# Hash attention and a Strassen-style squared-ReLU layer on one core: which queues carry the second part's transfers, and when they are asked for

## The chip, the cores and the metric

The kernel runs on one core of a Trainium2 chip. The metric is the device time of one execution in microseconds; less is better. Engines are named as in the profile: PE (TensorE), DVE (VectorE), ACT (ScalarE), POOL (GpSimd) and SP (SyncE). PEq, SPq and so on are their instruction queues. A transfer (DMA) is issued by an instruction in the queue of SP, ACT or POOL, in that queue's order, and is then carried out by 16 DMA engines.

## The reference

Attention over 4 x 8 heads of 768 tokens and 64 features, in which a query sees only the keys whose six sign bits equal its own, and then a layer with the square of a ReLU, all in fp32:

```python
q_bits = (np.einsum('bhsd,dk->bhsk', q, proj) > 0)      # the same for k
mask = q_bucket[:, :, :, None] == k_bucket[:, :, None, :]
scores = np.where(mask, scale * np.matmul(q, k.transpose(0, 1, 3, 2)), -1e9)
attn = softmax(scores)
x = (attn @ v).transpose(0, 2, 1, 3).reshape(3072, 512)
h = x @ w_in                                            # w_in 512 x 2048
g = np.maximum(h, 0.0) ** 2
out = g @ w_out                                         # w_out 2048 x 512
```

## The kernel before

**First part** (lines 542 to 596, 0 to 372 us): attention, 16 pairs of heads by 6 key tiles. Its results go to DRAM as `x_all`. Beside it the weights are rounded and stored in DRAM: `w_in_7` holds the seven Strassen factors of `w_in`, `w_out_1` the plain rows of `w_out`. The first chunk of tokens, `x`, is loaded back during this part (`load_x(0)` at step 54), and its sums `t_x` are made.

**Second part** (lines 599 to 942): three chunks of 1024 tokens. A chunk has eight **units** (`hidden`, one for 256 of the 2048 hidden features) and then a **projection** (`project`). A unit is one Strassen product of seven adds (`product`, line 612): 28 matmuls of 512 columns out of the unit's weights `w_unit` (896 KB, two buffers), with ACT copying three intermediate sums out of PSUM (`keep`: one, two, five, three) and DVE making the four squared outputs (`gate`). A projection is seven outer products, each again a Strassen product of seven adds: 49 adds of 8 matmuls of 256 columns, 392 in all. Each add reads a block of factors of 128 x 4 x 128, a **leaf** of 256 KB, loaded six ahead into eight buffers (`load_leaf`, line 753).

The 49 leaves come from `w_out_49` in DRAM, which is made during the first four units of chunk 0: `sums_out(m)` (line 888) loads 1 MB of `w_out_1` into `rows`, ACT copies three quarters of it to `factors`, DVE makes four more quarters and four times seven sums out of them (`sums_a`, line 477), and seven transfers of 448 KB store them. In chunks 1 and 2 each unit also takes the largest absolute value of a sixteenth of q and of k (`peak`, line 652: one buffer `raw_qk`, a load and a reduction, for q and then for k). The maxima set a flag, `slow` (`guard`, line 671), that selects a general version behind the end of the kernel; it isn't taken here.

**What sets the order.** Lines 542 on are under a manual schedule: each engine gets its instructions in the order of the Python code. All loads and stores of the second part stand in SP's queue, in program order, and SP waits at an instruction until its buffers are free and its data is there. So in a unit of chunk 0 SP has: the load of the unit after next (which waits until PE is through with this unit), the load of `rows`, and the seven stores. In chunks 1 and 2 it has the two loads of `raw_qk`, each of which waits for the reduction of the one before; at the last unit the first leaves stand behind them. Between leaves it has the stores of the output, four for each finished block (`put_out`, line 778). At the end of a chunk the next `x` is loaded ahead of the projection, and `sums_x` (line 530, four DVE operations) follows the projection.

Of the kernel before, what the change touches and what calls it, by code (L numbers as in the profile page):

```python
# [8 lines left out]
FP32 = mybir.dt.float32  # L9
# [25 lines left out]
def kernel(  # L35
# [10 lines left out]
    nc = tc.nc  # L46
# [50 lines left out]
    p_c = fast.enter_context(tc.tile_pool(name="p_c", bufs=1, side="right"))  # L97
    ps_s = first.enter_context(tc.tile_pool(name="ps_s", bufs=1, space=PSUM))
# [425 lines left out]
    def load_x(i):  # L524

        x = p_c.tile([P, NFT, NCH], FP32, name="x")
        nc.sync.dma_start(out=x, in_=x_all[:, :, i * NCH:(i + 1) * NCH])
        xs[i] = x, [p_c.tile([P, 2, NCH // 2], FP32, name=f"t_x{n}") for n in range(3)]

# [12 lines left out]
    with tc.manual_schedule():  # L542
# [14 lines left out]
        for u in range(len(steps) + 1):  # L557
# [34 lines left out]
            for f, i in w_steps.get(u, ()):  # L592
                f(i)
            if u == X_0:
                load_x(0)
# [4 lines left out]
        p_i = fast.enter_context(tc.tile_pool(name="p_i", bufs=2, reuse_waits="tile"))  # L600
# [48 lines left out]
        NPK = 16  # L649
        peaks = p_k.tile([P, 2, NPK], FP32, name="peaks")  # L650

        def peak(w, i):

            n = B * H * S * D // P // NPK
            t = p_k.tile([P, n], FP32, name="raw_qk")
            flat = (q, k)[w].rearrange("b h s d -> (b h s d)").rearrange("(p f) -> p f", p=P)
            nc.sync.dma_start(out=t, in_=flat[:, i * n:(i + 1) * n])
            nc.vector.tensor_reduce(  # L658
                out=peaks[:, w, i:i + 1], in_=t, axis=AXL.X, op=ALU.max,
# [28 lines left out]
        w_unit = {}  # L688

        def load_unit(n):  # L690

            if n < NCHUNK * NR:
                r = n % NR
                w_unit[n] = p_i.tile([P, 7, NFT // 2, P], FP32, name="w_unit")
                nc.sync.dma_start(
                    out=w_unit[n].rearrange("p l f c -> p (l f) c"),
                    in_=w_in_7.rearrange("p l f c -> p (l f) c")[:, :, r * P:(r + 1) * P],
                )

        def hidden(i, r):  # L700
# [11 lines left out]
            def gate(out):  # L712
                def put(one, two=None):
                    h = p_r.tile([P, HN], FP32, name="h", bufs=4)
# [38 lines left out]
        def load_leaf(n):  # L753
            if n < 49:
# [3 lines left out]
                nc.sync.dma_start(out=leaves[k, m], in_=w_out_49[OUTER[k][0], :, m])  # L758

        LEAVES, NLEAF = (0, 1, 4, 3, 5, 6, 2), 8  # L760
# [30 lines left out]
        def project(i):  # L791
# [54 lines left out]
            for k in range(7):  # L846
# [27 lines left out]
                )  # L874
                if k == 0:
# [11 lines left out]

        def sums_out(m):

            t = p_1.tile([P, 2, 2, 2, 2, P], FP32, name="rows")  # L890
# [251 lines left out]
```

## Time and profile before

| | us |
|---|---|
| Three runs, median (lowest to highest) | 1024.74 (1024.43 to 1025.59) |
| The profiled execution, whole | 1024.79 |
| Its span in the profile | 1022.9 |
| PE busy | 921.2 (90% of the span) |
| DVE busy | 700.0 (68%) |
| ACT busy | 371.1 (36%) |
| POOL busy | 6.0 (1%) |
| Queue 1 (SP's transfers) | 157.32 MB, 59.3% of 16 engines' span |

The profile is one execution. The profiled time is 1.9 us above its span, and 0.05 us above the median of the runs. The 40-slice view of the span shows PE at nine tenths or more in the first part, from slice 2 to slice 14, and at six tenths in slices 15 to 19, most of chunk 0 of the second part. There the granted TensorE clock is at seven and eight tenths of full speed. A busy PE at half clock is busy twice as long for the same work, so the busy share alone doesn't show the loss; the time of a stage beside the time of the same work at full pace does.

### The profile page before, as it was taken

Reading aid. Unit: us, or ns where it says so; the run is one execution under the profiler, and the core shown is the slowest. Engines: PE = TensorE matmul, PEld = TensorE weight load, DVE = VectorE, ACT = ScalarE, POOL = GpSimd, SP = SyncE. Lnnn points to the kernel's source line nnn. Section 1 sums busy time; section 2 is a strip of 40 time slices with the busy share of each in tenths; the row PEclk is TensorE's granted clock in tenths of the full one; section 3 lists DMA queues with packets and bytes.
Section 4 is the critical chain, followed back from the end, with each engine's and each line's share of the span. In section 5 each row is a group of like instructions: output and inputs, shape, how many; then the busy total and the mean of one; then the engine's idle time right before and its main releaser. Section 6 shows DMA issues by size and latency. Waiting matters only on the chain.

```text
span 1022.9 us, 11731 instructions
## 1 busy us (share of the span) xinstructions
PE 921.2 (90%) x4326; PEld 502.0 (49%) x4326; DVE 700.0 (68%) x1016; ACT 371.1 (36%) x607; POOL 6.0 (1%) x22
## 2 busy tenths in 40 slices
PE   5999999999999966666979998999599999978995
PEld 2334334334334422222448884444488744437884
DVE  2788977998867844544557875657677756676775
ACT  3777776777776712111211111222011122221110
POOL 2000000000000000000000000000000000000000
PEclk9999999999999978777989999999799999998998
DMA  9456885897663233777366563444854735526555
GB/s 185 102 105 134 237 172 108 225 232 202 152 143 109 88 108 108 231 217 226 102 211 192 154 149 86 136 147 133 286 152 131 156 85 154 153 67 194 151 151 109
DMA packets 287007, 158.14 MB, mean 155 GB/s; under 512 B 178016, under 2 KB 250208, under 8 KB 286944
## 3 DMA queue, kind: packets, MB, share of 16 engines
q1 hardware_dynamic: 286880, 157.32, 59.3%
q8 instruction: 36, 0.59, 0.2%
q14 instruction: 27, 0.22, 0.1%
q0 software_dynamic: 64, 0.00, 0.0%
HBM read 119.28 MB, written 38.01 MB: 154 GB/s over the span
## 4 chain that ended last, share of the span: by engine, by line
PE 66%; DMA 19%; DVE 9%; issue 2%; ACT 2%; SPq 2%; DVEq 0%; ACTq 0%
PE acc L621 33%; PE st L381 16%; PE xo L409 13%; DMA raw_qk<-in_q_dram 7%; DMA raw_qk<-in_k_dram 4%; DMA rows<-w_out 3%; PE tot L427 2%; DVE peaks L658 2%; DMA leaf<-w_out 2%; PE hash L322 2%; SPq L786 1%; DVE b L484 1%; DVE h L718 1%; DVE ot L782 1%; DVE t_x L484 1%
## 5 line engine op out<-in xcount | busy, mean ns | idle before, releaser
L386 ACT ACTIVATE e<-st 128x1024 f32<-128x1024 f32 x192 | 145.5, 810 | 90.9 <-PE st L381 90.4
L621 PE MATMUL acc<-x,w_unit 128*128 128x512 f32 x384 | 170.7, 596 | 8.2 <-DMA w_unit<-w_in 8.2
L621 PE MATMUL acc<-t_x,w_unit 128*128 128x512 f32 x288 | 139.1, 636 | 36.4 <-ACT one L628 33.8
L621 PE MATMUL acc<-b,leaf 128*128 128x256 f32 x600 | 138.5, 390 | 28.5 <-DMA leaf<-w_out 28.5
L381 PE MATMUL st<-feat,feat 64*128 64x512 f32 (+1 forms) x768 | 152.6, 489 | 0.0
L409 PE MATMUL xo<-e,v_nat 128*64 128x512 f32 (+1 forms) x768 | 144.9, 498 | 0.2 <-DVE x_t L464 0.2
L621 PEld LDWEIGHTS acc<-b,leaf 128*128 128x128 f32 x600 | 117.5, 196 | 47.8 <-DMA leaf<-w_out 31.0
L621 PEld LDWEIGHTS acc<-x,w_unit 128*128 128x128 f32 x384 | 73.4, 192 | 99.6 <-issue 98.8
L621 PEld LDWEIGHTS acc<-t_x,w_unit 128*128 128x128 f32 x288 | 58.4, 205 | 114.2 <-issue 73.8
L409 PEld LDWEIGHTS xo<-e,v_nat 128*64 128x64 f32 x768 | 46.9, 136 | 86.5 <-issue 84.8
L381 PEld LDWEIGHTS st<-feat,feat 64*128 64x128 f32 x768 | 67.3, 191 | 35.1 <-issue 32.5
L399 DVE TENSOR_TENSOR total<-total,e 128x1536 f32<-128x1536 f32 x48 | 83.7, 1744 | 1.1 <-ACT e L386 1.0
L628 ACT COPY one<-acc 128x512 f32<-128x512 f32 (+1 forms) x45 | 21.9, 486 | 153.9 <-PE acc L621 137.4
L658 DVE TENSOR_REDUCE peaks<-raw_qk 128x1 f32<-128x768 f32 x32 | 30.5, 953 | 68.4 <-DMA raw_qk<-in_k_dram 49.9
L621 PE MATMUL acc<-t,leaf 128*128 128x256 f32 x336 | 75.9, 379 | 0.0
L628 ACT COPY two<-acc 128x512 f32<-128x512 f32 (+1 forms) x45 | 21.9, 487 | 140.3 <-PE acc L621 137.3
L381 PE MATMUL st<-bits,bits 64*128 64x256 bf16 (+1 forms) x384 | 64.2, 331 | 7.4 <-DVE bits L347 5.4
L332 ACT ACTIVATE bits<-hash,lifts 32x384 bf16<-32x384 f32 x120 | 68.7, 573 | 4.9 <-PE hash L322 3.4
L621 PEld LDWEIGHTS acc<-t,leaf 128*128 128x128 f32 x336 | 63.8, 190 | 8.7
L719 DVE SCALAR_TENSOR_TENSOR b<-h 128x512 f32<-128x512 f32 x96 | 64.3, 690 | 2.5
L621 PE MATMUL acc<-b_t,leaf 128*128 128x256 f32 x240 | 54.5, 380 | 6.3 <-DMA leaf<-w_out 6.3
L381 PEld LDWEIGHTS <-bits 64*128 64x128 bf16 x384 | 19.0, 94 | 72.5 <-issue 65.8
(117 smaller groups left out, 808.9 us busy)
## 6 DMA issues: line engine op xcount, KB each, us to landing
leaf<-w_out SPq DMA_DIRECT2D x147, 256.0 KB, 2.8
w_unit<-w_in SPq DMA_DIRECT2D x24, 896.0 KB, 5.4
raw<-in_moe_w_in_dram SPq DMA_DIRECT2D x16, 512.0 KB, 4.3
raw<-in_moe_w_out_dram SPq DMA_DIRECT2D x16, 512.0 KB, 3.7
w_out<-sums SPq DMA_DIRECT2D x16, 448.0 KB, 6.0
v_nat<-in_v_dram SPq DMA_DIRECT2D x16, 384.0 KB, 4.2
x_all<-x_t SPq DMA_DIRECT2D x16, 384.0 KB, 3.0
x<-x_all SPq DMA_DIRECT2D x3, 2048.0 KB, 9.8
```

What stands on the lines that cost most here:

```text
L322: nc.tensor.matmul(out=hashed[pr][h][g * NR_B:(g + 1) * NR_B, 0:HS], lhsT=projs[rows], rhs=feat[pr, w][rows, c * HS:(c + 1) * HS], start=T ...
L332: nc.scalar.activation(out=t[h * D:h * D + NR_B, c * HS:(c + 1) * HS], in_=hashed[pr][h][at, 0:HS], func=ACTF.Sign, scale=HUGE, bias=lifts ...
L381: nc.tensor.matmul(out=st[:, h, 0:hi - lo], lhsT=src[pr, 1][rows, key], rhs=src[pr, 0][rows, lo:hi], start=first, stop=not first,)
L386: nc.scalar.activation(out=e[:, :, lo:hi], in_=st[:, :, 0:hi - lo], func=ACTF.Exp, scale=scale)
L399: nc.vector.tensor_tensor(out=totals[pr], in0=in0, in1=weights[pr, kt][:, :, 0:S], op=ALU.add)
L409: nc.tensor.matmul(out=xo[h * D:(h + 1) * D, lo:hi], lhsT=nat[pr, "v_nat"][:, h, kt * D:(kt + 1) * D], rhs=weights[pr, kt][:, h, lo:hi], s ...
L427: nc.tensor.matmul(out=tot[g * 32:(g + 1) * 32, 0:HS], lhsT=ones, rhs=src[:, h, c * HS:(c + 1) * HS], start=src is totals[pr], stop=src is ...
L484: nc.vector.tensor_tensor(out=out, in0=in0, in1=in1, op=ALU.subtract)
L621: nc.tensor.matmul(out=acc[to], lhsT=a(i), rhs=b(i), start=first and i == 0, stop=last and i == n - 1, skip_group_check=True,)
L628: nc.scalar.copy(out=t, in_=acc[of])
L658: nc.vector.tensor_reduce(out=peaks[:, w, i:i + 1], in_=t, axis=AXL.X, op=ALU.max, apply_absolute_value=True,)
L719: nc.vector.scalar_tensor_tensor(out=out[:, r], in0=h, scalar=0.0, in1=h, op0=ALU.max, op1=ALU.mult)
```

## The change

- The loads of `x`, the stores to `w_out_49` and the loads of `raw_qk` move from SP's queue to POOL's. The loads of leaves move to ACT's queue.
- The buffers `w_unit` are given room from the start, and units 0 and 1 are loaded during the first part, at step 60. The load of the unit after next stands at the end of a unit's work.
- `sums_out` no longer loads `rows` and has ACT copy three quarters of it. `load_rows` has four transfers put the quarters where they are needed (three into `factors`, one into `other`), with two buffers, for m and m + 1 ahead; m + 2 is asked for behind `sums_out(m)`.
- The maxima of q and k are taken in 32 pieces instead of 16, q and k in one buffer and one reduction, two pieces a unit, each loaded two ahead.
- The first five leaves are asked for one unit earlier (at r = 6). Leaves have seven buffers instead of eight, and `h` three instead of four.
- The next `x` is loaded behind the first outer product of the projection, and `sums_x` stands behind the sixth and the seventh one. `guard` stands behind the sixth.

```diff
     def load_x(i):
         x = p_c.tile([P, NFT, NCH], FP32, name="x")
-        nc.sync.dma_start(out=x, in_=x_all[:, :, i * NCH:(i + 1) * NCH])
+        nc.gpsimd.dma_start(out=x, in_=x_all[:, :, i * NCH:(i + 1) * NCH])
...
+            if u == X_0 + SB:
+                for n in range(2):
+                    load_unit(n)
             if u == X_0:
                 load_x(0)
...
-        NPK = 16
+        NPK = 32
...
+        def load_peak(i):
             n = B * H * S * D // P // NPK
-            t = p_k.tile([P, n], FP32, name="raw_qk")
-            flat = (q, k)[w].rearrange("b h s d -> (b h s d)").rearrange("(p f) -> p f", p=P)
-            nc.sync.dma_start(out=t, in_=flat[:, i * n:(i + 1) * n])
+            raw_qk[i] = p_k.tile([P, 2, n], FP32, name="raw_qk", bufs=2)
+            for w in range(2):
+                flat = (q, k)[w].rearrange("b h s d -> (b h s d)").rearrange("(p f) -> p f", p=P)
+                nc.gpsimd.dma_start(out=raw_qk[i][:, w], in_=flat[:, i * n:(i + 1) * n])
+
+        def peak(i):
+
             nc.vector.tensor_reduce(
-                out=peaks[:, w, i:i + 1], in_=t, axis=AXL.X, op=ALU.max,
+                out=peaks[:, :, i], in_=raw_qk.pop(i), axis=AXL.X, op=ALU.max,
...
-                nc.sync.dma_start(out=leaves[k, m], in_=w_out_49[OUTER[k][0], :, m])
+                nc.scalar.dma_start(out=leaves[k, m], in_=w_out_49[OUTER[k][0], :, m])
-        LEAVES, NLEAF = (0, 1, 4, 3, 5, 6, 2), 8
+        LEAVES, NLEAF = (0, 1, 4, 3, 5, 6, 2), 7
...
+                if k == 0 and i + 1 < NCHUNK:
+                    load_x(i + 1)
+                if k > 4 and i + 1 < NCHUNK:
+                    sums_x(i + 1, k - 5)
+                if k == 5 and i + 1 == NCHUNK:
+                    guard()
...
+        def load_rows(m):
+
+            f = p_1.tile([P, 7, 2, 2, P], FP32, name="factors")
+            t = p_1.tile([P, 2, 2, P], FP32, name="other")
+            src = w_out_1[:, m:NFF:NQ].rearrange("p n (h c) -> p n h c", h=2)
+            for o, n, h in ((f[:, 0], 0, 0), (f[:, 1], 2, 0), (t, 0, 1), (f[:, 2], 2, 1)):
+                nc.sync.dma_start(out=o.rearrange("p n h c -> p n (h c)"), in_=src[:, n:n + 2, h])
+            rows[m] = f, t
+
         def sums_out(m):
...
-            for n, a in enumerate((a11, a12, a22)):
-                nc.scalar.copy(out=f[:, n], in_=a)
-            sums_a(a11, a12, a21, a22, *(f[:, 3 + n] for n in range(4)))
-            g = p_1.tile([P, 4, 7, P], FP32, name="sums")
+            f, t = rows.pop(m)
+            sums_a(f[:, 0], f[:, 1], t, f[:, 2], *(f[:, 3 + n] for n in range(4)))
+            g = p_1.tile([P, 4, 7, P], FP32, name="sums", bufs=1)
...
-                nc.sync.dma_start(
+                nc.gpsimd.dma_start(
                     out=w_out_49[:, :, n, m].rearrange("l p e -> p l e"), in_=a
                 )
...
-        p_1 = p_1s.enter_context(tc.tile_pool(name="p_1", bufs=1, reuse_waits="tile"))
+        p_1 = p_1s.enter_context(tc.tile_pool(name="p_1", bufs=2, reuse_waits="tile"))
+        for m in range(2):
+            load_rows(m)
         for i in range(NCHUNK):
             for r in range(NR):
                 hidden(i, r)
-                load_unit(i * NR + r + 2)
                 minus(b_t[:, r], b12[:, r], b11[:, r])
                 if i == 0 and r < NQ:
                     sums_out(r)
-                if i > 0:
-                    for n in range(2):
-                        peak(n, (i - 1) * NR + r)
+                    if r + 2 < NQ:
+                        load_rows(r + 2)
...
-                if r == NR - 1:
+                if r == NR - 2:
                     for n in range(NLEAF - 2):
                         load_leaf(n)
+                load_unit(i * NR + r + 2)
+                for n in range(2):
+                    m = 2 * ((i - 1) * NR + r) + n
+                    if m >= 0:
+                        peak(m)
+                    if 0 <= m + 2 < NPK:
+                        load_peak(m + 2)
```

How the instructions stand, at three places. A name in brackets behind `waits` is a semaphore: DMAHW0 to 7 count the transfers issued by SP and ACT together, DMASW0 to 7 those issued by POOL, the others name an engine.

SP's queue at the beginning of the second part, before: the three loads of weights, the first load of `rows`, the stores of m = 0 and the next unit and rows:

```order
L695 DMA w_unit<-w_in_63 128x14x128 [waits DMAHW5_49]
L695 DMA w_unit<-w_in_63 128x14x128 [waits DMAHW6_49]
L695 DMA w_unit<-w_in_63 128x14x128 [waits DMAHW7_49,DMAHW5_49,PE_49]
L891 DMA rows<-w_out_65 128x4x512 [waits DMAHW0_49,Activation_49]
L903 DMA w_out_66<-factors 128x7x128 [waits DMAHW1_49,DVE_49,Activation_49]
L903 DMA w_out_66<-factors 128x7x128 [waits DMAHW2_49]
L903 DMA w_out_66<-factors 128x7x128 [waits DMAHW3_49]
L903 DMA w_out_66<-sums 128x7x128 [waits DMAHW4_49,DVE_49]
L903 DMA w_out_66<-sums 128x7x128 [waits DVE_49]
L903 DMA w_out_66<-sums 128x7x128 [waits DMAHW6_49]
L903 DMA w_out_66<-sums 128x7x128 [waits DMAHW7_49,DVE_49]
L695 DMA w_unit<-w_in_63 128x14x128 [waits DMAHW0_49,PE_49]
```

The same queue in the changed kernel, from the third load of quarters (m = 2) on; the quarters of m = 0 and 1 stand right ahead of it:

```order
L909 DMA factors<-w_out_65 128x2x256 [waits DMAHW1_49,DMASW5_49,DMAHW6_49,DMASW4_49,DMAHW7_49,DMASW3_49,DVE_49]
L909 DMA factors<-w_out_65 128x2x256
L909 DMA other<-w_out_65 128x2x256 [waits DMAHW0_49]
L909 DMA factors<-w_out_65 128x2x256
L538 DMA w_unit<-w_in_63 128x14x128 [waits DMAHW2_49,PE_49]
L909 DMA factors<-w_out_65 128x2x256 [waits DMASW4_49,DMAHW3_49,DMASW3_49,DMAHW5_49,DMASW2_49,DVE_49]
L909 DMA factors<-w_out_65 128x2x256 [waits DMAHW4_49]
L909 DMA other<-w_out_65 128x2x256
L909 DMA factors<-w_out_65 128x2x256 [waits DMAHW6_49]
L538 DMA w_unit<-w_in_63 128x14x128 [waits DMAHW7_49,PE_49]
L538 DMA w_unit<-w_in_63 128x14x128 [waits DMAHW2_49,DMAHW0_49,PE_49]
```

The stores are gone from the queue and the loads of m = 2 and 3 stand ahead of the loads of units 2 and 3; the first of each four waits for three transfers that POOL issued.

POOL's queue, before, from its last work of the first part to the read of the flag at the end:

```order
L249 TENSOR_TENSOR picks<-ident 128x32 x4
L252 MEMSET which 128x24
L254 MEMSET which 32x12 [waits Pool_49]
L254 MEMSET which 32x12 x3
L971 TENSOR_LOAD slow [waits DVE_49]
```

In the changed kernel, the same place and the stores of m = 0 (the first three are those of `factors`, the other four those of `sums`):

```order
L255 MEMSET which 32x12 x3
L528 DMA x<-x_all 128x4x1024 [waits DMAHW7_49,DMAHW3_49]
L920 DMA w_out_66<-factors 128x7x128 [waits DMAHW6_49,DMAHW7_49,DMAHW1_49,DVE_49]
L920 DMA w_out_66<-factors 128x7x128 x2
L920 DMA w_out_66<-sums 128x7x128 [waits DVE_49] x2
L920 DMA w_out_66<-sums 128x7x128 [waits DMASW0_49]
L920 DMA w_out_66<-sums 128x7x128 [waits DMASW1_49,DVE_49]
L920 DMA w_out_66<-factors 128x7x128 [waits DMAHW3_49,DMAHW2_49,DMAHW5_49,DMASW2_49,DVE_49]
L920 DMA w_out_66<-factors 128x7x128 [waits DMASW3_49]
```

A queue that was empty in the second part now has 28 stores in chunk 0, in groups of seven, and after them the loads of `raw_qk` and `x`.

ACT's queue at the beginning of the first projection, before: the last copy of unit 7 and then the copies of the first two outer products:

```order
L716 COPY h<-acc_3643 128x512 [waits DVE_49,PE_49]
L628 COPY one<-acc_3708 128x256 [waits PE_49]
L628 COPY two<-acc_3708 128x256 [waits PE_49]
L628 COPY five<-acc_3710 128x256 [waits PE_49]
L628 COPY three<-acc_3708 128x256 [waits PE_49]
L812 COPY sum_3704<-acc_3708 128x256 [waits DMAHW2_49,DMAHW6_49,DMAHW1_49,DMAHW7_49,DMAHW0_49,PE_49]
L628 COPY one<-acc_3778 128x256 [waits DVE_49,PE_49]
L628 COPY two<-acc_3778 128x256 [waits DVE_49,PE_49]
L628 COPY five<-acc_3780 128x256 [waits DVE_49,PE_49]
```

The same place in the changed kernel:

```order
L765 DMA leaf<-w_out_66 128x512 [waits DMAHW3_49,DMASW7_49,DMASW6_49]
L643 COPY one<-acc_3707 128x256 [waits PE_49,Activation_49]
L765 DMA leaf<-w_out_66 128x512 [waits DMAHW4_49]
L765 DMA leaf<-w_out_66 128x512 [waits DMAHW5_49]
L643 COPY two<-acc_3707 128x256 [waits PE_49,Activation_49]
L765 DMA leaf<-w_out_66 128x512 [waits DMAHW6_49]
L643 COPY five<-acc_3709 128x256 [waits PE_49,Activation_49]
L765 DMA leaf<-w_out_66 128x512 [waits DMAHW7_49]
L643 COPY three<-acc_3707 128x256 [waits PE_49,Activation_49]
L765 DMA leaf<-w_out_66 128x512 [waits DMAHW0_49]
L765 DMA leaf<-w_out_66 128x512 [waits DMAHW1_49]
L819 COPY sum_3703<-acc_3707 128x256 [waits PE_49]
```

The leaves stand between the copies that PE waits for, and wait for counters that SP's transfers use too.

## Rows read from the trace of the kernel before

**Rows 1.** The page, its first line.

```profile
span 1022.9 us, 11731 instructions
```

**Rows 2.** Busy time of each engine in six stretches, us; then granted clock, DMA share, GB/s.

```profile
371.90:529.80 157.90, 109.85 (x224) 46.88 (x225) 79.79 (x118) 29.66 (x52) 0.00 (x0) 0.83 0.59 173
529.80:618.40 88.60, 86.59 (x393) 75.69 (x394) 63.08 (x88) 11.17 (x30) 0.00 (x0) 0.98 0.65 182
618.40:727.50 109.10, 96.48 (x225) 42.23 (x223) 68.91 (x102) 23.44 (x40) 0.00 (x0) 0.97 0.46 134
727.50:816.30 88.80, 86.81 (x393) 75.90 (x394) 65.03 (x93) 11.18 (x30) 0.00 (x0) 0.98 0.66 182
816.30:925.00 108.70, 96.37 (x224) 42.12 (x223) 68.71 (x102) 23.46 (x40) 0.00 (x0) 0.97 0.41 117
925.00:1014.50 89.50, 87.08 (x394) 75.87 (x394) 65.26 (x95) 11.19 (x30) 0.00 (x0) 0.98 0.62 159
```

**Rows 3.** What TensorE waited for: us in total, times, longest.

```profile
PE acc L621 <- DMA leaf<-w_out: 34.9, 6, 11.4
...
PE acc L621 <- ACT one L628: 33.8, 4, 9.0
...
PE acc L621 <- DMA w_unit<-w_in: 8.2, 1, 8.2
```

**Rows 4.** Chain of waits from 364 to 530: start us, us, what.

```profile
371.45 0.42 PE tot L451 x2
...
380.04 13.67 PE acc L621 x28
...
394.34 8.39 DMA rows<-w_out
...
475.84 47.88 PE acc L621 x104
```

**Rows 5.** The same chain, of the whole span.

```profile
529.80 72.66 PE acc L621 x328
...
632.66 5.98 DMA raw_qk<-in_q_dram
```

**Rows 6.** TensorE in order of time: start, us, line, operation, idle before and releaser.

```profile
405.00 7.97 PE L621 MATMUL acc<-t_x,w_unit 128*128 128x512 f32 x12 [7.87 <-ACT one L628]
...
727.54 2.93 PE L621 MATMUL acc<-b,leaf 128*128 128x256 f32 x6 [11.37 <-DMA leaf<-w_out]
```

**Rows 7.** Busy time from 394 to 464, columns as in rows 2.

```profile
394.00:464.00 70.00, 44.56 (x85) 18.69 (x84) 37.31 (x52) 13.18 (x24) 0.00 (x0) 0.78 0.73 218
```

**Rows 8.** VectorE from 372 to 420 in order of time.

```profile
403.36 0.68 DVE L479 TENSOR_TENSOR factors<-rows 128x512 f32<-128x512 f32 x1
...
406.49 1.09 DVE L479 TENSOR_TENSOR sums<-factors 128x896 f32<-128x896 f32 x1
```

**Rows 9.** DMA issues: queue, count, KB each, median us from issue to landing.

```profile
rows<-w_out SPq DMA_DIRECT2D x4, 1024.0 KB, 8.8
...
w_out<-sums SPq DMA_DIRECT2D x16, 448.0 KB, 6.0
...
w_out<-factors SPq DMA_DIRECT2D x12, 448.0 KB, 4.3
...
leaf<-w_out SPq DMA_DIRECT2D x147, 256.0 KB, 2.8
```

**Rows 10.** DMA issuing instructions of lines 903, 758 and 224: ns min/median/max.

```profile
L903 SPq DMA_DIRECT2D w_out<-sums x16: 1311/1386/1711, 407.7 to 482.9; - x16
...
L758 SPq DMA_DIRECT2D leaf<-w_out x147: 319/320/897, 524.4 to 1009.5; - x147
...
L224 POOL DMA_DIRECT2D projs<-in_proj_dram x2: 522/592/662, 1.7 to 2.4; - x2
```

**Rows 11.** SyncE from 1000 to 1023, and a piece of the chain near it.

```profile
1004.97 4.38 SPq L786 DMA_DIRECT2D out_dram<-ot  x8
...
1003.66 1.99 DMA out_dram<-ot
```

## What was predicted

> **What bounds the kernel now.** The first view is busy time by stage. The second part is six stretches in which PE has the same work three times over: eight units and a projection, for each of three chunks. The first stretch takes 157.9 us where the third and fifth take 109.1 and 108.7 for the same eight units; the projections take 88.6, 88.8 and 89.5 [rows 2]. The second view, the chain of waits, gives the pace without waits: four units in a row in 47.88 us, or 11.97 a unit, and six of the seven outer products of a projection in 72.66 us, or 12.11 each [rows 4, 5]. At that pace eight units are 95.8 us and a projection 84.8, and the second part 3 x (95.8 + 84.8) = 541.8 us. The six stretches are 642.6 us long [rows 2], so 100.8 us are lost: 62.1, 3.8, 13.3, 4.0, 12.9 and 4.7, in their order. This is the most that the change can win; the first part it hardly touches.
>
> What ends the waits, PE's list of them tells: leaves 34.9 us, ACT's copy "one" 33.8 us, the first unit's weights 8.2 us [rows 3]. The middle one isn't ACT's doing. In the chain the load of `rows` comes ahead of it, 8.39 us from 394.34 on, after unit 0 (13.67 us from 380.04 on) was through [rows 4]: SP's queue had the load of unit 2, which waits for unit 0, ahead of `rows`. ACT waits with its copies of `rows`, and the copy "one" that PE needs stands behind them; PE sat idle for 7.87 us before 405.00 [rows 6]. The rest of these 62.1 us is clock: between 394 and 464 the granted clock was 0.78 [rows 7], a mixture of 1.2 and 2.4 GHz after each wait, and unit 0, started after 8.2 us of waiting, took 13.67 us and not 11.97, so a restart costs 1.7 us.
>
> **The change, part by part.**
>
> *Start of chunk 0.* Units 0 and 1 are in place early, so PE may go on after its last product of the first part, which ends at 371.45 + 0.42 = 371.87 [rows 4]. I leave 0.5 us of 8.2, and the clock stays up. In the first part two more loads of 896 KB lie beside work bound by PE, at no cost.
>
> *Units 0 to 3.* ACT's twelve copies go, and the quarters of m = 0 and 1 are loaded before they are needed. But the quarters of m = 2 stand ahead of unit 2's weights in SP's queue and wait until the three `factors` stores of m = 0 have landed. This is the new wait on PE's path. DVE is through with unit 0's gates some 2 us after 384.4; four sums of 0.68 us follow, then four of 1.09 [rows 8]. So the first three stores can be issued at about 389.
>
> What POOL takes to issue one, p, no row shows. The only transfers of POOL took 0.52 and 0.66 us for 64 rows each; a store has 896 pieces, which in proportion is 14 x 0.59 = 8.3 us. SP's issue of the same store took 1.39 us [rows 10]. This is the same transfer, so the nearest row: I take p = 1.4 and keep 0.6 and 8.3 as ends. The Trainium skill ("DMA: Bandwidth & Descriptors", section "Anatomy of one DMA — SWDGE (gpsimd) path") says that POOL's software path can emit many descriptors before their cost shows; no run here shows it yet. That speaks for the low end, with which the sum would be 2.4 us lower.
>
> Three issues end at 393.2, and the last store lands 4.3 us later [rows 9], at 397.5. Four quarters are issued in 4 x 0.32 = 1.3 us (the issue of a leaf, also 256 KB [rows 10]), then unit 2's weights, which land with the quarters in about the 8.8 us that `rows` took beside a unit [rows 9]: 407.6. PE wants them after two units, at 396.3. That is a wait of 11.3 us and 1.7 for the restart. Unit 2 ends at 421. For m = 1 the same steps from 401 give 401 + 4.2 + 4.3 + 1.3 + 8.8 = 419.6 for unit 3's weights: just in time. No quarters stand ahead of later units. DVE's load is 37.31 us in three units, 12.4 each [rows 7], a little above 11.97, and costs about 1 us over four units, the rest being buffered. In all 0.5 + 11.3 + 1.7 + 1 = 14.5 us are left of 62.1, the leaf wait at the chunk's end among what goes, since the leaves are asked for a unit earlier and stand behind no other queue.
>
> *Units of chunks 1 and 2.* PE already keeps pace there; what is lost lies at the end, where the first leaves stand behind the loads of `raw_qk` in SP's queue (a piece of 5.98 us in the chain, one of many [rows 5]): PE waited 11.37 us [rows 6]. On ACT the leaves are free of that. DVE still has two reductions and the last inner sums between the last gate and the third add of the projection; I leave 1.5 us of 13.3 and of 12.9. POOL's four loads a unit, two units ahead, are hidden even at several us each.
>
> *Projections.* The sums of `x` no longer stand between projection and unit, and the cold start goes. But ACT now waits, ahead of copies, for counters shared with SP's output stores. In the last two outer products eight stores take 4.38 us to issue and 1.99 to land [rows 11], behind some 3 us of DVE; PE's cover is three adds of 12.11 / 7 = 1.73 us [rows 5]. That is 4.4 + 2.0 + 3 - 5.2 = 4.2 at most and zero at least; with a little left at the start I take 3.5 each, against 3.8, 4.0 and 4.7. A leaf's issue of 0.32 us, 49 times, is 16 us of an ACT that is busy for 11.2 of 88.6 us [rows 2].
>
> *Sum.* 14.5 + 2 x 1.5 + 3 x 3.5 = 28.0 us remain of 100.8, a gain of 72.8. The profiled execution took 1024.8 us (1022.9 of span [rows 1] and 1.9 around it), within 0.1 of the median, so 1024.8 - 72.8 = **952.0**.
>
> **Rivals.** *POOL is slow.* From 395 (389 and the last landing, 6.0 [rows 9]) all 28 stores take 28 p; ACT meets the first leaves after unit 6 and waits there for all of them, with unit 7's copies behind. Chunk 0 then ends at 395 + 28 p + 13. The forecast has it at 371.9 + 95.8 + 14.5 = 482, so up to p = 2.7 this costs little; at p = 4 it ends at 520, for 990 us. Break-even with before is 482 + 72.8 = 555, or p = 5.25. At 8.3 it ends at 640: **1110 us, slower**. For it speaks the proportion to the 64-row loads, against it SP's 1.39 us.
>
> *The 16 engines are the bound.* From 394 to 464 three units' transfers kept them busy for 0.73 of 70 us [rows 7], 17.0 us a unit, where PE needs 11.97. If they fill up, units 0 to 3 end at 372.4 + 68 = 440.4 and not 433.4: 959 us. The Trainium skill ("DMA: Bandwidth & Descriptors", "Issuing engines are not separate DMA queues") says that several issuing queues share the same engines and save only issue time. By that rule this rival has the upper hand; the trace agrees that the engines weren't full, at 0.73.
>
> *ACT is held up by leaves.* If all nine leaf loads of the last two outer products wait 2.0 us each in turn, a projection loses 18 us and not 3.5: 995 us. Against it: loads and copies alternate, and most stores are long done.
>
> **How the numbers follow.** The forecast has 0.66, with a range of its own from 932 (hardly a stall left in chunk 0) to 972 (twice the stall); the engines as the bound 0.10; POOL between 2.7 and 5.25 us 0.10; ACT held up 0.05; POOL above that 0.09. The range of 930 to 990 leaves out the slow POOL (0.09), part of the middling one and of ACT held up (0.06) and 0.04 of the forecast. Faster is 0.89, within 0.2% (what a measurement of this kernel can tell from no change) 0.02, slower 0.09.
>
> **What would show it.** The stretch of chunk 0 tells most: some 110 us from the first unit to the projection, with one wait of PE for `w_unit` before unit 2 and no wait for ACT's "one". POOL's issue of a store should be near 1.4 us. The waits for leaves at the start of a projection should be gone, and what is left at its end should name ACT. The forecast is wrong if POOL's stores take over 2.7 us each, if PE waits for weights before units 3 to 5 too, or if the granted clock in chunk 0 stays below 0.9.

## The result, and the profile after

The changed kernel takes 955.64 us (953.94 to 956.22), the kernel before in the same session 1024.59: a ratio of 0.9327, 95% interval 0.9308 to 0.9345. Forecast were 952.0 and a range of 930 to 990. The profiled execution took 956.22 us, 1.7 of it around its span.

The page of the changed kernel: its first line, TensorE's line, and in the slices PE and the granted clock.

```profile
span 954.5 us, 11820 instructions
...
PE 904.1 (95%) x4326; PEld 493.7 (52%) x4326; DVE 696.9 (73%) x1016; ACT 364.5 (38%) x595; POOL 69.2 (7%) x117
...
PE   5999999999999999549999999999999999999996
...
PEclk8999999999999999869999999999999999999998
```

Where before five slices stood at six tenths, two at five and four are left, the 17th and 18th: one hole instead of many. The six stretches, cut at the same events as in [rows 2] (columns as there):

```profile
371.20:496.40 125.20, 98.81 (x225) 42.66 (x224) 75.10 (x111) 22.72 (x39) 29.01 (x32) 0.90 0.69 208
496.40:581.70 85.30, 84.91 (x393) 74.23 (x392) 68.12 (x96) 11.75 (x31) 0.76 (x1) 1.00 0.67 190
581.70:678.50 96.80, 96.62 (x226) 42.43 (x225) 63.01 (x98) 22.82 (x39) 14.85 (x28) 1.00 0.50 143
678.50:764.10 85.60, 85.04 (x393) 74.27 (x392) 69.79 (x98) 11.75 (x31) 2.86 (x5) 1.00 0.70 198
764.10:860.40 96.30, 96.30 (x225) 42.47 (x225) 62.95 (x98) 22.82 (x39) 14.87 (x28) 1.00 0.47 134
860.40:945.90 85.50, 85.29 (x395) 74.30 (x393) 68.82 (x102) 11.75 (x31) 0.00 (x0) 1.00 0.59 155
```

At the pace of the prediction (95.8 and 84.8) they lose 29.4, 0.5, 1.0, 0.8, 0.5 and 0.7 us: 32.9 in all, against 100.8 before and 28.0 forecast. Everything after the units of chunk 0 runs at full clock and within 1.1% of the pace. Nearly all that is left is one wait. First two rows of TensorE's waits (us in total, times, longest), then the row of TensorE in order of time in which the longest ends:

```profile
PE acc L636 <- DMA w_unit<-w_in: 25.1, 3, 24.4
...
PE acc L636 <- ACT one L643: 1.4, 3, 0.8
```

```profile
419.72 5.17 PE L636 MATMUL acc<-x,w_unit 128*128 128x512 f32 x8 [24.45 <-DMA w_unit<-w_in]
```

There is no wait for a leaf any more, and ACT's "one" is down from 33.8 to 1.4 us [rows 3]. The wait of 24.45 us is for unit 2. With the restart (8 matmuls in 5.17 us, elsewhere 3.60) it makes 26.0 of chunk 0's 29.4. The chain of waits tells how it came about (start us, us, what):

```profile
388.42 1.91 POOL w_out L920 x2
390.33 6.01 DMA w_out<-factors
...
401.00 18.67 DMA w_unit<-w_in
...
419.72 37.80 PE acc L636 x84
```

and SP's queue in order of time beside it:

```profile
377.41 20.94 SPq L909 DMA_DIRECT2D factors<-w_out  x3
398.40 1.25 SPq L909 DMA_DIRECT2D other<-w_out  x1
399.69 1.21 SPq L909 DMA_DIRECT2D factors<-w_out  x1
401.00 1.39 SPq L538 DMA_DIRECT2D w_unit<-w_in  x1
```

This is the predicted order, step by step: stores of m = 0 by POOL, their landing, the quarters of m = 2 in SP's queue, and only then unit 2's weights. The load itself took 18.67 us, where 8.8 were forecast. The DMA queues between 401.0 and 419.7 (packets, MB, share of the 16 engines' time) show what it shared the engines with:

```profile
q0 software_dynamic: 1002, 3.55, 59.1%
q1 hardware_dynamic: 3659, 2.70, 44.5%
```

The engines were full. POOL's transfers (q0) had three fifths of them, in packets of 3.5 KB, while SP's transfers went in packets of 0.7 KB (2.70 MB / 3659).

### The profile page after: what moved, and what is told of

It reads as the page before. It is cut to its first block, busy times and chain, and to the rows that moved or that the text cites. A ratio compares the mean times of both kernels' runs of the same rounds, so it can differ in the third digit from the quotient of the medians.

```text
span 954.5 us, 11820 instructions
## 1 busy us (share of the span) xinstructions
PE 904.1 (95%) x4326; PEld 493.7 (52%) x4326; DVE 696.9 (73%) x1016; ACT 364.5 (38%) x595; POOL 69.2 (7%) x117
## 4 chain that ended last, share of the span: by engine, by line
PE 88%; DMA 5%; DVE 3%; ACT 1%; issue 1%; SPq 1%; ACTq 0%; POOL 0%; DVEq 0%
PE acc L636 52%; PE st L382 17%; PE xo L410 14%; DMA w_unit<-w_in 3%; PE tot L428 2%; PE hash L323 2%; DMA w_out<-factors 1%; PE tot L452 1%; DVE b L726 1%; ACT bits L333 0%; SPq L909 0%; ACT e L387 0%; DMA k_nat<-in_k_dram 0%; DVE h L725 0%; DVE peaks L677 0%
## 5 line engine op out<-in xcount | busy, mean ns | idle before, releaser
L636 PE MATMUL acc<-b,leaf 128*128 128x256 f32 x600 | 133.0, 379 | 0.0
L636 PE MATMUL acc<-t_x,w_unit 128*128 128x512 f32 x288 | 128.0, 594 | 1.4 <-ACT one L643 1.4
L636 PEld LDWEIGHTS acc<-b,leaf 128*128 128x128 f32 x600 | 113.8, 190 | 17.0 <-issue 1.4
L410 PEld LDWEIGHTS xo<-e,v_nat 128*64 128x64 f32 x768 | 46.9, 136 | 86.5 <-issue 84.8
L636 PEld LDWEIGHTS acc<-t_x,w_unit 128*128 128x128 f32 x288 | 54.3, 190 | 71.9 <-issue 66.3
L725 DVE TENSOR_TENSOR h<-acc,two 128x512 f32<-128x512 f32 x24 | 16.6, 690 | 88.3 <-PE acc L636 88.3
```

Source lines behind the costliest of these rows:

```text
L410: nc.tensor.matmul(out=xo[h * D:(h + 1) * D, lo:hi], lhsT=nat[pr, "v_nat"][:, h, kt * D:(kt + 1) * D], rhs=weights[pr, kt][:, h, lo:hi], s ...
L636: nc.tensor.matmul(out=acc[to], lhsT=a(i), rhs=b(i), start=first and i == 0, stop=last and i == n - 1, skip_group_check=True,)
L725: nc.vector.tensor_tensor(out=h, in0=one, in1=two, op=ALU.add)
```

## The experiments

| Kernel | us, median (lowest to highest) | Ratio to before, 95% interval |
|---|---|---|
| changed kernel | 955.64 (953.94 to 956.22) | 0.9327 (0.9308 to 0.9345) |
| u1_stores_on_sp | 960.78 (959.53 to 962.03) | 0.9371 (0.9347 to 0.9395) |
| u2_leaves_on_sp | 975.51 (974.51 to 976.51) | 0.9514 (0.9492 to 0.9537) |
| u3_peaks_on_sp | 988.16 (986.61 to 989.71) | 0.9646 (0.9624 to 0.9669) |
| u4_units_late | 969.32 (968.83 to 969.81) | 0.9462 (0.9444 to 0.9481) |
| u5_sumsx_late | 961.39 (959.13 to 962.06) | 0.9362 (0.9343 to 0.9382) |
| e1_unit_first | 946.88 (945.89 to 947.64) | 0.9232 (0.9216 to 0.9248) |
| e2_rows_on_pool | 952.35 (950.53 to 953.92) | 0.9292 (0.9270 to 0.9314) |
| e3_whole_rows | 940.19 (937.84 to 942.43) | 0.9179 (0.9157 to 0.9202) |
| e4_whole_rows_pool | 939.39 (936.20 to 942.09) | 0.9160 (0.9131 to 0.9189) |
| e5_seven_sums | 946.47 (946.02 to 946.97) | 0.9226 (0.9210 to 0.9242) |
| e6_seven_sums_pool | 929.92 (929.78 to 932.95) | 0.9072 (0.9050 to 0.9094) |
| e7_seven_sums_short | 950.86 (950.34 to 953.47) | 0.9276 (0.9252 to 0.9300) |

The first five take one part of the change back. The others ask why unit 2 waited and what stood behind that.

### Parts taken back

**u1_stores_on_sp**: the 28 stores to `w_out_49` stay in SP's queue.

```diff
-                nc.gpsimd.dma_start(
+                nc.sync.dma_start(
                     out=w_out_49[:, :, n, m].rearrange("l p e -> p l e"), in_=a
```

> One part of the change undone: the 28 stores go back to SP's queue, everything else as in the changed kernel. If a free queue for the stores matters, it is by what stands behind them: unit 2 is late as before (within 3 us), and units 4 and 5 stand behind stores that wait for DVE until some 448 and 463, so PE waits about 12 us for each: 970 to 985. If only the engines' bandwidth matters, the bytes are the same and the time stays within 4 us of 955.6.

Measured: 5.1 us slower than the changed kernel, less than the one text asks for and more than the other. Two of TensorE's rows in order of time, and the DMA queues from 401.4 to 408.9, where unit 2's load was under way:

```profile
408.93 6.03 PE L636 MATMUL acc<-x,w_unit 128*128 128x512 f32 x8 [12.92 <-DMA w_unit<-w_in]
...
445.18 6.68 PE L636 MATMUL acc<-x,w_unit 128*128 128x512 f32 x8 [7.63 <-DMA w_unit<-w_in]
```

```profile
q1 hardware_dynamic: 3750, 2.40, 111.6%
```

Without a rival queue unit 2's load took 7.5 us and the wait was 12.92: close to the forecast's 8.8 and 11.3. So the forecast had priced the load as if the stores were still in SP's queue. What the stores cost there comes later: unit 4's load stands behind those of m = 2 and goes out only at 436.73, for the wait of 7.63. Moving the stores to POOL exchanged one wait for another and won 5 us.

**u2_leaves_on_sp**: the leaves stay in SP's queue, still asked for a unit earlier.

```diff
-                nc.scalar.dma_start(out=leaves[k, m], in_=w_out_49[OUTER[k][0], :, m])
+                nc.sync.dma_start(out=leaves[k, m], in_=w_out_49[OUTER[k][0], :, m])
```

> One part undone: the leaves go back to SP's queue, still asked for a unit earlier and without loads of q and k in that queue. If those loads were what held the first leaves, only the waits at the end of each projection come back, behind output stores, 2.0 to 2.4 us each, with a little clock: 960 to 965. If the queue itself holds the leaves, the waits of 6 to 11 us at the start of the projections come back as well: 978 or more.

Measured: 19.9 us slower, between the two. SP's queue, and the first of TensorE's waits:

```profile
485.31 12.53 SPq L538 DMA_DIRECT2D w_unit<-w_in  x2
497.94 57.90 SPq L765 DMA_DIRECT2D leaf<-w_out  x34
```

```profile
508.63 7.14 PE L636 MATMUL acc<-b,leaf 128*128 128x256 f32 x32 [2.70 <-DMA leaf<-w_out]
```

Five leaves are out early, but the sixth stands behind the load of unit 9, which goes out only when PE is through with unit 7, at the end of the first row; in chunk 0 that costs PE the wait of 2.70. It is the smaller part of 14.8 us in eight pieces. The other seven, 12.1 us, lie in the last two outer products of the projections, where leaves stand behind eight stores of the output. SP's queue and one of these waits of PE:

```profile
578.41 4.42 SPq L793 DMA_DIRECT2D out_dram<-ot  x8
582.93 0.93 SPq L765 DMA_DIRECT2D leaf<-w_out  x2
```

```profile
585.97 5.20 PE L636 MATMUL acc<-b_t,leaf 128*128 128x256 f32 x16 [2.88 <-DMA leaf<-w_out]
```

So with the loads of `raw_qk` out of SP's queue, it is the output stores that hold the leaves up there, as the first text has it, by more than it forecast.

**u3_peaks_on_sp**: the maxima of q and k as before, in 16 pieces, one buffer, SP's queue.

```diff
-        NPK = 32
+        NPK = 16
...
-                nc.gpsimd.dma_start(out=raw_qk[i][:, w], in_=flat[:, i * n:(i + 1) * n])
+            t = p_k.tile([P, n], FP32, name="raw_qk")
+            nc.sync.dma_start(out=t, in_=flat[:, i * n:(i + 1) * n])
...
+                if i > 0:
+                    for n in range(2):
+                        peak(n, (i - 1) * NR + r)
```

> One part of the change undone: q and k are loaded in SP's queue again, into one buffer, a load and a reduction in turn, 16 pieces each. The leaves stay on ACT. If the wait of 11.4 us that PE had at the start of two projections came only from leaves behind those loads, it stays away: 957 to 960. If DVE, held by the loads, was as late as the leaves, PE waits for DVE's inner sums instead, about 8 us and a restart of 1.7 in each of two chunks: 970 to 978.

Measured: 32.5 us slower, more than either text. A row of the chain, and TensorE's longest wait:

```profile
679.61 13.12 DMA raw_qk<-in_q_dram
```

```profile
698.73 4.64 PE L636 MATMUL acc<-t,leaf 128*128 128x256 f32 x10 [14.88 <-DVE t L485]
```

The leaves, on ACT, came in time. It is DVE that stood still, at a reduction that waited for its load, with the sums that PE needs queued behind. The loads come one after the other, since there is one buffer and SP issues each behind that of a unit. This one took 13.12 us, where no load of `raw_qk` took over 6.4 in the kernel before: POOL had issued the 2 MB of the next `x` at 679.25. From 679.6 to 692.7 the DMA queues were

```profile
q0 software_dynamic: 528, 2.10, 41.6%
q1 hardware_dynamic: 1952, 1.31, 31.8%
q10 hardware_dynamic: 432, 0.79, 16.3%
```

At the end of chunk 2, where no `x` follows, the same wait of PE is 5.26 us. That the transfer of `x` stretched the load is read from these rows; no run moves `x` alone. A slow DVE stood behind the leaf in [rows 6] too, unnamed since the leaf came later still. This row of VectorE in the kernel before is the first of the sums `t` behind the last reduction:

```profile
727.67 0.41 DVE L484 TENSOR_TENSOR t<-b 128x256 f32<-128x256 f32 x1
```

It began 0.1 us after the leaf had come, at 727.54. With the leaf early, PE would have gone on at 716.2, done two adds of 1.73 us and waited for the second of these sums until about 728.5. By this estimate the leaves alone, moved to ACT, would have won some 2.5 of the 11.37 us; by u3's chunk 2, with 5.26 in place of 11.06 us, some 6. No run tries it on the kernel before.

**u4_units_late**: units 0 and 1 are loaded after the first part.

```diff
-            if u == X_0 + SB:
-                for n in range(2):
-                    load_unit(n)
...
         NOUT = 2
+        for n in range(2):
+            load_unit(n)
```

> One part undone: units 0 and 1 are loaded at the beginning of the second part, in SP's queue ahead of the quarters. My step: PE's wait of 8.2 us and its restart of 1.7 come back, and the quarters come some 2 us later: 964 to 968. Rival: these waits are swallowed by the later wait before unit 2, which the quarters and stores set: 956 to 960.

Measured: 13.7 us slower, a little above the first text.

```profile
380.52 6.74 PE L633 MATMUL acc<-x,w_unit 128*128 128x512 f32 x8 [8.40 <-DMA w_unit<-w_in]
...
431.69 6.77 PE L633 MATMUL acc<-x,w_unit 128*128 128x512 f32 x8 [23.83 <-DMA w_unit<-w_in]
```

The start wait is that of [rows 3] again, and the 8 matmuls after it take 6.74 us instead of 3.60: 11.5 of the 13.7. Unit 2's wait moves along unchanged, so the early loads neither caused nor eased it.

**u5_sumsx_late**: `sums_x` behind the whole projection again.

```diff
-                if k > 4 and i + 1 < NCHUNK:
-                    sums_x(i + 1, k - 5)
...
+            if i + 1 < NCHUNK:
+                for n in range(2):
+                    sums_x(i + 1, n)
```

> The changed kernel with sums_x behind the whole projection again, one part undone; the load of x stays behind the first outer product. If the four sums of x at the boundary hold up the first unit of chunks 1 and 2, as the prediction has it (3.8 and 4.0 us lost in a projection before, 0.5 and 0.8 after): 957 to 962, with a wait of PE of 1.3 to 3 us at the start of each of those two units. If PE's time at the boundary came back by the earlier leaves alone: 954.5 to 956.5.

Measured: in the first range; by the ratios 0.0035 or 3.6 us, though the two intervals overlap. PE has the wait that was looked for:

```profile
PE acc L636 <- DVE t_x L485: 3.9, 2, 1.9
```

### Why unit 2 waits

**e1_unit_first**: the load of a unit stands ahead of the quarters in SP's queue.

```diff
                     sums_out(r)
-                    if r + 2 < NQ:
-                        load_rows(r + 2)
+                load_unit(i * NR + r + 2)
+                if i == 0 and r + 2 < NQ:
+                    load_rows(r + 2)
...
-                load_unit(i * NR + r + 2)
```

> One change to the changed kernel: in SP's queue the weights of units 2 and 3 stand ahead of the quarters of m = 2 and 3, instead of behind them. Theory A (the order in SP's queue causes the 24.4 us wait before unit 2): unit 2's weights are asked for when PE is through with unit 0, at 383, and land by 392; the wait before unit 2 goes with its restart, some 26 us. Unit 3's weights now stand behind the quarters of m = 2, are asked for near 401 and may be 5 to 10 us late. In all 936 to 943. Rival B (the 16 engines are full, so the bytes of units, quarters and stores set the pace whatever their order): the wait moves to unit 3 or 4 or to DVE, and less than 8 us come back: 948 to 956.

Measured: 8.8 us faster than the changed kernel, between the two ranges. Unit 2's load goes out at 383.05 and its wait is gone. Unit 3's, behind the quarters of m = 2, takes 18.5 us:

```profile
419.62 6.14 PE L636 MATMUL acc<-x,w_unit 128*128 128x512 f32 x8 [12.57 <-DMA w_unit<-w_in]
```

The place in the queue was half of it; the slowness of the load is still there.

**e2_rows_on_pool**: the quarters of m = 2 and 3 go to POOL's queue; SP has nothing but loads of units.

```diff
-        def load_rows(m):
+        def load_rows(m, queue=nc.sync):
...
-                        load_rows(r + 2)
+                        load_rows(r + 2, nc.gpsimd)
```

> One change to the changed kernel: the quarters of m = 2 and 3 are asked for in POOL's queue, behind the stores whose landing they wait for, so SP's queue has nothing but units. Theory A: units 2 and 3 are asked for at 383 and 395, as soon as PE frees their buffers, and PE has no wait over 3 us in chunk 0; the stretch of chunk 0 shrinks from 125.2 to 98 to 103 us, 930 to 935 in all. Rival B (engines full): at 17.0 us of the engines' time a unit, units 0 to 3 can't end before 371.2 + 68 = 439, and the stretch stays at 114 us or more: 944 or more.

Measured: 3.3 us faster than the changed kernel by the medians, though the two intervals overlap, and in rival B's range: the theory of the queue's order alone fell. Unit 3's load is asked for as soon as its buffer is free and has no other transfer ahead of it in its queue, and it takes 27.7 us:

```profile
423.47 5.17 PE L636 MATMUL acc<-x,w_unit 128*128 128x512 f32 x8 [15.78 <-DMA w_unit<-w_in]
```

**e3_whole_rows** and **e4_whole_rows_pool**: e1 and e2 with the factors of `w_in` laid out unit by unit in DRAM, so that a unit's load consists of rows of 7 KB instead of pieces of 512 B. The bytes are the same; the first part stores them with another pattern.

```diff
-    w_in_7 = p_d.tile([P, 7, NFT // 2, HF], FP32, name="w_in_7")
+    w_in_7 = p_d.tile([P, NR, 7, NFT // 2, P], FP32, name="w_in_7")
...
-                out=w_unit[n].rearrange("p l f c -> p (l f) c"),
-                in_=w_in_7.rearrange("p l f c -> p (l f) c")[:, :, r * P:(r + 1) * P],
+                out=w_unit[n].rearrange("p l f c -> p (l f c)"),
+                in_=w_in_7[:, r].rearrange("p l f c -> p (l f c)"),
```

> The kernel of e1_unit_first with one more change: the factors of w_in lie in DRAM unit by unit, so a unit's load reads 7 KB in one piece a partition and no longer 14 pieces of 512 B; bytes, queues and order are those of e1. Theory C (the two queues take turns packet by packet, and POOL's packets of some 3.6 KB take the engines from SP's packets of 512 B): the load of unit 3 lands in under 10 us instead of 18.4, PE's wait of 12.6 us before it falls to under 3, and the whole takes 933 to 938. Rival B (the engines are full, and a share doesn't depend on the size of packets): that load still takes over 14 us, and the time stays at 943 to 947.

> The same layout in the kernel of e2_rows_on_pool, where SP's queue has units alone. Theory C: unit 3's load, 27.7 us in e2, falls to under 10 us, PE's wait of 15.8 us goes, and the time is 932 to 937; DVE, which then waits for quarters and stores, may give 2 to 4 us back. Rival B: the load stays above 20 us and the time at 949 to 953.

Measured: 6.7 and 13.0 us faster than e1 and e2. The longest load of a unit takes 10.1 and 10.8 us, not 18.5 and 27.7 (theory C asks for under 10). Both times lie about 2 us above the range of theory C, since something else was late next. One row of TensorE in order of time and one of the chain, of e3_whole_rows:

```profile
445.83 5.42 PE L643 MATMUL acc<-t_x,w_unit 128*128 128x512 f32 x12 [2.77 <-ACT one L650]
```

```profile
411.10 9.83 DMA w_out<-sums
```

DVE waits for the one buffer `sums` until the last store of the quarter before has landed; the next unit's gates stand behind, and so do ACT and PE.

**e5_seven_sums** and **e6_seven_sums_pool**: e3 and e4 with seven small buffers for the sums instead of one large one.

```diff
-            g = p_1.tile([P, 4, 7, P], FP32, name="sums", bufs=1)
+            g = [p_1.tile([P, 7, P], FP32, name="sums", bufs=7) for n in range(4)]
```

> e3_whole_rows (940.2), but the four second-level sums of a quarter have buffers of their own, seven of 3.5 KB in place of one of 14 KB, so that DVE needn't wait for the last store of the quarter before. Theory S: in e3_whole_rows the next thing late is DVE, which waits 11.5 us in three waits for that one buffer and then has PE wait some 6.5 us for units 3 and 4. Without it 931 to 936, and no wait of DVE for a store of sums. Theory T: the DMA engines are what is late, and the wait only moves, to unit weights or to factors: 938 to 942.

> The same seven buffers in e4_whole_rows_pool (939.4), where the quarters of m = 2 and 3 are asked for by POOL behind the stores. Theory S: 930 to 935, PE's waits for ACT's one (7.8 us in four) down to some 2. Theory T: 937 to 941.

Measured: the same edit made e3 6.3 us slower (4.8 by the ratios) and e4 9.5 us faster. The first lies above the ranges of both theories, the second 0.1 us below that of theory S. In e6_seven_sums_pool the hole is closed, as theory S has it. Its stretches of chunk 0 (columns as in [rows 2]) and the one wait of PE in it over 0.3 us:

```profile
371.50:469.30 97.80, 96.36 (x225) 42.22 (x224) 74.80 (x111) 22.76 (x39) 35.27 (x40) 1.00 0.82 266
469.30:554.70 85.40, 84.95 (x394) 74.51 (x393) 68.29 (x96) 11.77 (x31) 0.76 (x1) 1.00 0.67 190
```

```profile
436.01 5.42 PE L643 MATMUL acc<-t_x,w_unit 128*128 128x512 f32 x12 [1.15 <-ACT one L650]
```

Chunk 0 is 2.0 us above its pace, against 62.1 before [rows 2]. In e5_seven_sums DVE waits for no store either, but the quarters are still in SP's queue. SP and then TensorE in order of time:

```profile
418.50 31.07 SPq L545 DMA_DIRECT2D w_unit<-w_in  x3
```

```profile
435.06 5.57 PE L643 MATMUL acc<-x,w_unit 128*128 128x512 f32 x8 [10.57 <-DMA w_unit<-w_in]
```

Unit 4's load could have gone at 406.7, when PE was through with unit 2, but stands behind the quarters of m = 3 until 418.50. It did in e3_whole_rows too, at the same 418.50, and was there by 427.3. Now the stores of m = 2 are issued 6 to 8 us earlier, right beside it, and it takes 16.5 us. The quarters ahead of it in SP's queue land late as well (the three of `factors` after a median of 11.8 us, 7.4 in e3_whole_rows). So it seems that DVE's wait had kept those stores out of the way; no run moves them alone.

**e7_seven_sums_short**: e6 with the old layout of `w_in_7`, so that only the size of the pieces differs.

```diff
-                out=w_unit[n].rearrange("p l f c -> p (l f c)"),
-                in_=w_in_7[:, r].rearrange("p l f c -> p (l f c)"),
+                out=w_unit[n].rearrange("p l f c -> p (l f) c"),
+                in_=w_in_7.rearrange("p l f c -> p (l f) c")[:, :, r * P:(r + 1) * P],
```

> e6_seven_sums_pool (929.9) with the weights of a unit in their old place in DRAM, in rows of 512 B and not 7 KB; so the one difference between the two is the size of the rows that SP's loads of units consist of, and the one difference from e2_rows_on_pool (952.4) the seven buffers of the sums. Theory C: while POOL's queue has stores or quarters to carry, a load in rows of 512 B gets little of the DMA engines. Then unit 3's load again takes over 20 us, PE waits over 10 us for it, and the time is 947 to 957, no better than e2_rows_on_pool. Theory D: the wait in e2_rows_on_pool came from the one buffer of the sums, which stretched the stores: landing under 12 us, no wait for w_unit over 3 us, 930 to 937.

Measured: 20.9 us slower than e6, in theory C's range. Unit 3's load takes 27.5 us, unit 4's 28.2, and PE waits 15.59 before unit 3. The DMA queues from 407.3 to 415.3, while SP's load of unit 4 is under way in both kernels, first of e7_seven_sums_short, then of e6_seven_sums_pool:

```profile
q0 software_dynamic: 728, 2.59, 87.7%
q1 hardware_dynamic: 728, 0.37, 15.5%
```

```profile
q0 software_dynamic: 598, 2.13, 71.6%
q1 hardware_dynamic: 141, 0.90, 30.1%
```

In e7 both queues moved 728 packets, POOL's of 3.6 KB and SP's of 0.5 KB: as many packets, a seventh of the bytes. In e6 SP's packets are 6.4 KB and its load is through in 9.3 us. The Trainium skill ("DMA: Bandwidth & Descriptors", section "Queues, rings and completion order") says that an engine takes turns between queues and switches at the end of a packet. The trace of e7 agrees in these 8 us, with 728 to 728, but not over a longer stretch, here from 395.2 to 422.8, from the start of unit 3's load to its landing:

```profile
q0 software_dynamic: 2031, 7.10, 81.3%
q1 hardware_dynamic: 2890, 1.47, 19.1%
```

Nor do 1002 to 3659 in the changed kernel or 141 to 598 in e6 agree with it. In the changed kernel SP's queue moved one packet from 396 to 401, beside 359 of POOL's, though the first quarter had been issued by 396.9. So the experiments show that the size of the pieces decides how soon the load is through beside POOL's transfers, and not by what rule the engines share themselves out.

## Why the prediction came out as it did

*What bounds the kernel* was right: 100.8 us were to be had, 67.9 are gone from the six stretches, and e6, at 929.9, is 95.9 below the kernel before in its session. For the start of the projections the list of waits named the leaf alone; behind it stood DVE, held up by `raw_qk` (u3).

*Start of chunk 0*: right. PE goes from the first part's last product into unit 0 at 371.15, and u4 prices the early loads at 13.7 us, 8.4 of them the wait.

*Units 0 to 3* is the step that was mis-sized: 29.4 us are left, not 14.5, and the stretch is 125.2 us and not some 110. The mechanism, order and place were as written (first stores issued at 388.4, forecast 389; last one landed at 396.3, forecast 397.5, with a landing of 6.01 us where 4.3 were taken). POOL's issue of a store took 1.0 us, below the 1.4 taken (the changed kernel's line 920: ns min/median/max, first and last start):

```profile
L920 POOL DMA_DIRECT2D w_out<-sums x16: 929/1050/1197, 391.2 to 460.3; - x16
L920 POOL DMA_DIRECT2D w_out<-factors x12: 929/986/1022, 388.4 to 453.1; - x12
```

Two terms failed. Unit 2's load took 18.67 us and not 8.8: its price came from [rows 9], where every transfer was in SP's one queue, and the change itself put a second queue beside it. The four quarters were issued in 4.4 us and not 1.3, a price from leaves [rows 10]; the second queue isn't the reason there, since with the stores in SP's queue (u1) they took 4.0, from 397.24 to 401.29. Of the 13.1 us by which the wait is longer, 9.9 are the load, 2.2 its later start, and 1.0 that PE was ready sooner. u1 gives the check for the load: stores in SP's queue again, and it takes 7.5 us.

*Units 3 on*: "just in time" held only because unit 2 was late; in e1, e2 and e7 the wait is at unit 3.

*Units of chunks 1 and 2*: 1.0 and 0.5 us are left, 1.5 each were taken. u2 and u3 show that both moves were needed, that of the leaves and the new scheme of the loads of `raw_qk`; in u2 the gain of the leaves' move lies mostly in the projections' ends.

*Projections*: 3.5 us each were taken, 0.5, 0.8 and 0.7 measured, so 8.5 us too much in all. The step that failed is ACT's wait for the output stores: it was priced at up to 4.2 us of PE's time, and it takes none. The profile does name such waits of ACT, 28.7 us in six, but the same idle time stands before the copy "one" in an outer product that has no stores. Two rows of the changed kernel's ACT, the first without and the second with output stores:

```profile
522.58 0.37 ACT L643 COPY one<-acc 128x256 f32<-128x256 f32 x1 [4.75 <-PE acc L636]
558.84 0.37 ACT L643 COPY one<-acc 128x256 f32<-128x256 f32 x1 [4.75 <-DMA out_dram<-ot]
```

ACT waits there for its turn in PE's pace, and the store named is only the last of several sources by the profile.

*The sum.* Chunk 0 lost 14.9 us more than forecast, the projections 8.5 and the units of chunks 1 and 2 1.5 us less. That the time came out 3.6 us from 952.0 is in good part luck: errors of opposite sign.

*The rivals.* POOL is slow: no, 1.0 us. ACT is held up by leaves: no wait of PE shows it. The 16 engines are the bound: they were full where PE waited, and the time lies between the forecast's and this rival's 959. But e6 carries the same bytes through chunk 0 in 97.8 us with the engines at 0.82, and is through with four units at about 419, where this rival has 440. The transfers themselves do take about as long as the rival says, since the engines are busy for 0.93 of the time from 383 to 445 in e6; but PE waits only for the loads of units among them. So full engines alone don't hold PE up; who gets them while they are full decides. The rule of the Trainium skill that the prediction weighed ("DMA: Bandwidth & Descriptors", section "Issuing engines are not separate DMA queues") says that several queues save only issue time. In u2 that time isn't small: eight stores of the output take 4.42 us of SP's queue to go out, and with what they wait for they hold up the leaves behind them; with the sixth leaf's wait at the start that cost 19.9 us. u3's 32.5 us are for the queue and the single buffer together. On the shared engines themselves the traces agree with that rule.

*Open*: by what rule the two queues share the engines; what the new `load_rows` is worth alone (the quarters put in place by transfers, ahead of time, and ACT's copies gone), since no run takes it back, though PE's waits for ACT's "one" fell from 33.8 to 1.4 us with it; and how the five parts' prices share what they have in common: they add up to 77.0 us by difference of medians, and the change won 69.

## What to carry to other kernels

Before a transfer moves to another queue, ask what stood behind it (that is the gain) and what it will now run beside (that is the price): a load priced from a trace where all was in one queue took twice to three times as long beside another queue's transfers. Give the load that the bound engine waits for long rows in DRAM, here 20.9 us for the same bytes (e6 against e7). When a wait is taken away, look for the transfer that it had kept apart from another: the same edit was worth 9.5 us with the queue cleared and cost 6.3 without. Before a wait is blamed on the source that the profile names, look whether it is there where that source isn't.

## What the runs showed of the hardware

- A store of 448 KB in 896 pieces of 512 B takes POOL 0.93 to 1.20 us to issue, about twice the 0.59 us for 64 rows of [rows 10]; the proportion to pieces (8.3 us) was far off.
- The same store's packets are 3.5 KB in POOL's queue (1002 packets, 3.55 MB, in the changed kernel), while pieces of 512 B issued by SP go as packets of 0.5 KB (728 packets, 0.37 MB, in e7).
- A unit's load lands in 5.2 us at the least in pieces of 512 B (e7) and in 4.4 us in rows of 7 KB (e6); beside POOL's transfers it takes up to 28.2 against 10.5. The size of the pieces costs little alone and much in company. Long rows don't help against what stands ahead in the load's own queue: behind four quarters it took 16.5 us in rows of 7 KB (e5).
- SP's issue of a quarter took about 0.5 us for m = 0 and 1 and mostly 1.2 to 1.4 for m = 2, beside POOL's stores. With the stores in SP's own queue (u1) it took 1.4 for the first two of m = 2 and 0.59 for the others.
